# Attention kept on chip, paired heads on both halves of the array, and token-major expert outputs

## The chip, the cores and the metric

One core of one Trainium2 chip. The metric is the device time of one execution in microseconds, the median of several runs. A second number is the span of one profiled execution, from its first to its last instruction.

## The reference, cut to what matters

Inputs are q, k, v of shape 8 x 12 x 448 x 64 (batch, heads, sequence, head size), two scale vectors of 64, a gate matrix (768 x 8), one dense pair of weights (768 x 512, 512 x 768) and eight expert pairs of the same shapes. Everything is float32.

```python
q_n, k_n = rmsnorm(q, g_q), rmsnorm(k, g_k)
attn = softmax(q_n @ k_n.T / sqrt(64))
x = (attn @ v), heads side by side, as (3584 tokens, 768)
y_dense = relu(x @ w1_dense) @ w2_dense
expert = argmax(x @ w_gate);  gate = softmax(x @ w_gate)[expert]
out = y_dense + gate * (relu(x @ w1[expert]) @ w2[expert])
```

Both kernels compute every expert for every token and weigh the result with the gate, which is zero for the experts not chosen.

## The kernel before

It has one function, in which the Tile framework sets the semaphores and orders each engine's queue by the order of the program and the buffers of the pools.

**Attention** (lines 90 to 144) goes batch by batch. For q and k of one batch (12 heads, 5376 rows, 42 rows on each of 128 partitions) it loads f32 (line 96), squares, sums, inverts and takes the root (lines 98 to 102), multiplies by the factor and by g (lines 105, 107), pads to 128 columns and writes bf16 to DRAM (line 109). v is only cast and written (lines 111 to 114). Then two transposing DMAs read q and k back with the head size on the partitions (lines 118, 119), and v comes back with a column of ones (lines 121, 122). For each head there are four score matmuls of 64 x 112 by 448 columns (line 131), each with an exponential on ScalarE (line 132), and for each of four blocks of 112 queries four matmuls of 112 x 112 weights by 65 columns (line 137), a copy out of PSUM (line 139), and the division by the sum in the 65th column (lines 141, 142). The batch's result goes to DRAM (line 144).

**Change-over and gate.** The result comes back transposed as `xc` (line 156). The gate matrix is the stationary operand, so the logits have experts on the partitions (line 161); maximum and sum over them are all-reduces on POOL (lines 166, 172); the gate goes to DRAM (line 179).

**Expert layers** (lines 182 to 220). For the dense pair and each expert, w1t and w2t are loaded through POOL's queue into a pool with one buffer (lines 186, 188). For each of seven blocks of 512 tokens, 24 matmuls make the hidden layer (line 200), which is rectified and multiplied by the gate (line 205; line 209 for the dense pair), and 24 more make the output with features on the partitions (line 214), which VectorE adds to `yacc` (line 220).

**Output** (lines 225 to 231). `yacc` is transposed in f32 in 168 blocks of 128 x 128, each copied (line 230) and written by a DMA of its own (line 231).

Of the kernel before, what the change touches and what calls it, by code (L numbers as in the profile page):

```python
# [14 lines left out]
RO = bass_isa.ReduceOp  # L15
# [3 lines left out]
def kernel(  # L19
# [16 lines left out]

# [4 lines left out]
    F = moe_w1_dense.shape[1]  # L41

    SC = 112
    NSC = S // SC
    scale = 1.0 / (D ** 0.5)
    KD = Dm // P
    NC = 512
    NNC = N // NC
    FT = F // P
    DT = Dm // P  # L50

    xbuf = nc.dram_tensor("x_scratch", (N, Dm), BF16).ap()
    DP = 128
    qn = nc.dram_tensor("qn_scratch", (B * H * S, DP), BF16).ap()
    kn = nc.dram_tensor("kn_scratch", (B * H * S, DP), BF16).ap()
    vn = nc.dram_tensor("vn_scratch", (B * H * S, D), BF16).ap()
    gmask = nc.dram_tensor("gmask_scratch", (E, N), F32).ap()

    const_pool = ctx.enter_context(tc.tile_pool(name="const", bufs=1))
    ident = const_pool.tile([P, P], BF16)  # L60
    make_identity(nc, ident)
    gq_t = const_pool.tile([SC, D], F32)
    gk_t = const_pool.tile([SC, D], F32)
    nc.sync.dma_start(gq_t, bass.AP(tensor=g_q.tensor, offset=g_q.offset, ap=[[0, SC], [1, D]]))
    nc.sync.dma_start(gk_t, bass.AP(tensor=g_k.tensor, offset=g_k.offset, ap=[[0, SC], [1, D]]))
    eps_t = const_pool.tile([P, 1], F32)
    nc.vector.memset(eps_t, 1e-6)

    gq_b = const_pool.tile([P, D], F32)
    gk_b = const_pool.tile([P, D], F32)  # L70
    nc.sync.dma_start(gq_b, bass.AP(tensor=g_q.tensor, offset=g_q.offset, ap=[[0, P], [1, D]]))
    nc.sync.dma_start(gk_b, bass.AP(tensor=g_k.tensor, offset=g_k.offset, ap=[[0, P], [1, D]]))
    BHS = B * H * S
    assert BHS % P == 0
    NBHS = BHS // P
    CH = H * S // P
    assert CH * P == H * S
    qv = q.rearrange("b h s d -> (b h s) d").rearrange("(c p) d -> p c d", p=P)
    kv = k.rearrange("b h s d -> (b h s) d").rearrange("(c p) d -> p c d", p=P)
    vv = v.rearrange("b h s d -> (b h s) d").rearrange("(c p) d -> p c d", p=P)  # L80
    qn_v = qn.rearrange("(c p) d -> p c d", p=P)
    kn_v = kn.rearrange("(c p) d -> p c d", p=P)
    vn_v = vn.rearrange("(c p) d -> p c d", p=P)
# [178 lines left out]
```

## Time and profile before

| | us |
|---|---|
| median of 3 runs (lowest, highest) | 1605.18 (1605.03, 1608.18) |
| span of the profiled execution | 1605.4 |
| TensorE matmuls busy | 1119.3 |
| VectorE busy | 712.4 |
| ScalarE busy | 327.6 |
| GpSimd busy | 97.5 |

Busy time is the union of an engine's instruction records. A matmul's record lasts longer than its share of the engine, because matmuls are pipelined, so the spacing of matmuls says more than their duration. PE is TensorE, PEld its weight loads, DVE VectorE, ACT ScalarE, POOL GpSimd, SP the engine that issues most DMAs. On the timeline and in the chain, a line merges a row of equal instructions: start, length from the first start to the last end, and how many.

### The profile page before, as it was taken

Reading aid. Unit: us, or ns where it says so; the run is one execution under the profiler, and the core shown is the slowest. Engines: PE = TensorE matmul, PEld = TensorE weight load, DVE = VectorE, ACT = ScalarE, POOL = GpSimd, SP = SyncE. Lnnn points to the kernel's source line nnn. Section 1 sums busy time; section 2 is a strip of 40 time slices with the busy share of each in tenths; the row PEclk is TensorE's granted clock in tenths of the full one; section 3 lists DMA queues with packets and bytes.
Section 4 is the critical chain, followed back from the end, with each engine's and each line's share of the span. In section 5 each row is a group of like instructions: output and inputs, shape, how many; then the busy total and the mean of one; then the engine's idle time right before and its main releaser. Section 6 shows DMA issues by size and latency. Waiting matters only on the chain.

```text
span 1605.4 us, 13421 instructions
## 1 busy us (share of the span) xinstructions
PE 1119.3 (70%) x5093; PEld 553.6 (34%) x5154; DVE 712.4 (44%) x1205; ACT 327.6 (20%) x747; POOL 97.5 (6%) x97
## 2 busy tenths in 40 slices
PE   0283719091826455375699989898989898989765
PEld 0151406050413333241244434343434343434322
DVE  6442524445262717120833646464646464645100
ACT  1242515151523334240441000000000000000333
POOL 0000000000000000001710000000000000000000
PEclk9999999999999999999899999999999999999655
DMA  8949394968869493819002020202020202020233
GB/s 175 194 84 173 64 190 86 183 110 156 136 110 182 78 210 51 144 18 177 2 2 40 1 40 1 40 1 40 1 40 1 40 1 40 1 40 1 82 97 97
DMA packets 394064, 125.49 MB, mean 78 GB/s; under 512 B 328656, under 2 KB 393936, under 8 KB 393992
## 3 DMA queue, kind: packets, MB, share of 16 engines
q1 hardware_dynamic: 381408, 110.47, 37.5%
q0 software_dynamic: 12592, 14.17, 6.0%
q8 instruction: 40, 0.66, 0.2%
q14 instruction: 24, 0.20, 0.0%
HBM read 67.11 MB, written 44.15 MB: 69 GB/s over the span
## 4 chain that ended last, share of the span: by engine, by line
PE 52%; DMA 23%; SPq 9%; DVE 7%; issue 4%; ACT 3%; POOL 2%; ACTq 0%; POOLq 0%; DVEq 0%
PE yp L214 17%; PE hp L200 16%; PE out_ps L137 10%; PE sc_ps L131 9%; DMA out_dram<-od 5%; DMA va<-vn_scratch 5%; SPq L118 4%; DMA w1t<-in_moe_w_dram 4%; DMA qn_scratch<-xn 4%; DMA w2t<-in_moe_w_dram 3%; SPq L119 3%; DVE xn L107 2%; DVE ssq L100 2%; SPq L156 2%; DVE xn L105 1%
## 5 line engine op out<-in xcount | busy, mean ns | idle before, releaser
L131 PE MATMUL sc_ps<-qTa,kTa 64*112 64x448 bf16 x384 | 197.7, 594 | 324.6 <-DMA kTa<-kn_scratch 318.7
L214 PE MATMUL yp<-ht,w2t 128*128 128x512 bf16 x1479 | 353.7, 386 | 30.7 <-ACT logits L164 11.2
L200 PE MATMUL hp<-xc,w1t 128*128 128x512 bf16 x1484 | 352.2, 385 | 30.8 <-DMA w1t<-in_moe_w_dram 28.9
L205 DVE SCALAR_TENSOR_TENSOR ht<-hp,gsc 128x512 bf16<-128x512 f32 x224 | 145.4, 686 | 240.6 <-PE yp L214 214.9
L220 DVE TENSOR_TENSOR yacc<-yacc,yp 128x512 f32<-128x512 f32 x336 | 205.9, 682 | 54.0 <-PE yp L214 54.0
L132 ACT ACTIVATE ex<-sc_ps 112x448 bf16<-112x448 f32 x384 | 189.7, 551 | 179.3 <-PE sc_ps L131 179.3
L200 PEld LDWEIGHTS <-w1t 128*128 128x128 bf16 x1512 | 149.9, 99 | 219.1 <-DMA w1t<-in_moe_w_dram 32.8
L214 PEld LDWEIGHTS <-w2t 128*128 128x128 bf16 x1512 | 148.6, 99 | 219.0 <-issue 39.8
L137 PE MATMUL out_ps<-va,ex 112*112 112x65 bf16 x1536 | 186.8, 284 | 31.4 <-DVE va L122 22.9
L137 PEld LDWEIGHTS <-ex 112*112 112x112 bf16 x1536 | 160.1, 206 | 130.9 <-issue 91.4
L230 ACT COPY od<-pT 128x128 f32<-128x128 f32 x168 | 44.2, 266 | 704.8 <-PE pT L228 639.9
L131 PEld LDWEIGHTS <-kTa 64*112 64x112 bf16 x384 | 61.6, 182 | 360.2 <-DMA kTa<-kn_scratch 319.7
L139 DVE COPY out_all<-out_ps 112x65 f32<-112x65 f32 x302 | 57.0, 221 | 163.2 <-PE out_ps L137 157.6
L228 PE MATMUL pT<-ident,yacc 128*128 128x128 f32 x168 | 74.2, 458 | 31.6 <-ACT od L230 29.8
L195 POOL PARTITION_BROADCAST gsc<-g x56 | 44.5, 796 | 492.9 <-DVE ht L205 483.9
L122 DVE MEMSET va<- 112x48 bf16 x8 | 0.8, 98 | 153.5 <-DMA va<-vn_scratch 153.5
L228 PEld LDWEIGHTS pT<-ident,yacc 128*128 128x128 f32 x168 | 29.8, 178 | 76.1 <-ACT od L230 74.0
L98 DVE TENSOR_TENSOR sq<-xt 128x2688 f32<-128x2688 f32 x16 | 47.1, 2941 | 10.2 <-DMA xt<-in_q_dram 10.2
L132 ACT ACT_TABLE_LOAD x8 | 10.3, 1283 | 190.5 <-PE sc_ps L131 190.4
L105 DVE TENSOR_TENSOR xn<-xt,ssq 128x2688 bf16<-128x2688 f32 x16 | 47.3, 2955 | 2.7 <-ACT ssq L102 2.7
L100 DVE TENSOR_REDUCE ssq<-sq 128x42 f32<-128x2688 f32 x16 | 47.1, 2945 | 0.1
L153 POOL DMA_DIRECT2D wgb<-in_moe_w_gate_dram x1 | 1.1, 1137 | 711.9 <-DMA x_scratch<-ob_a 711.9
(37 smaller groups left out, 342.3 us busy)
## 6 DMA issues: line engine op xcount, KB each, us to landing
qn_scratch<-xn SPq DMA_DIRECT2D x8, 1344.0 KB
kn_scratch<-xn SPq DMA_DIRECT2D x8, 1344.0 KB
out_dram<-od SPq DMA_DIRECT2D x168, 64.0 KB
w1t<-in_moe_w_dram POOLq DMA_DIRECT2D x8, 768.0 KB, 7.4
w2t<-in_moe_w_dram POOLq DMA_DIRECT2D x8, 768.0 KB, 6.9
vn_scratch<-xn SPq DMA_DIRECT2D x8, 672.0 KB
va<-vn_scratch SPq DMA_DIRECT2D x8, 672.0 KB
x_scratch<-ob_a SPq DMA_DIRECT2D x8, 672.0 KB
```

The source lines that it names most:

```text
L100: nc.vector.tensor_reduce(ssq, sq, AX.X, ALU.add)
L105: nc.vector.tensor_mul(xn[:, :, :D], xt, ssq.unsqueeze(2).to_broadcast([P, CH, D]))
L118: nc.sync.dma_start(qTa, qn3[b], transpose=True)
L131: nc.tensor.matmul(sc_ps, kT[:, j * SC:(j + 1) * SC], qT, start=True, stop=True)
L132: nc.scalar.activation(ex[:, j, :], sc_ps, AF.Exp, scale=scale)
L137: nc.tensor.matmul(out_ps, ex[:, j, mi * SC:(mi + 1) * SC], va[:, h, j, :], start=(j == 0), stop=(j == NSC - 1))
L139: nc.any.tensor_copy(out_all[:, mi, :], out_ps)
L200: nc.tensor.matmul(hp, w1t[:, kk, ff * P:(ff + 1) * P], xc[:, kk, nj * NC:(nj + 1) * NC], start=(kk == 0), stop=(kk == KD - 1))
L205: nc.vector.scalar_tensor_tensor(ht, in0=hp, scalar=0.0, in1=gsc, op0=ALU.max, op1=ALU.mult)
L214: nc.tensor.matmul(yp, w2t[:, ff, dd * P:(dd + 1) * P], hts[ff], start=(ff == 0), stop=(ff == FT - 1))
L220: nc.vector.tensor_add(ysl, ysl, yp)
L228: nc.tensor.transpose(pT, yacc[:, dd, nn * P:(nn + 1) * P], ident32)
```

## The change

Attention no longer goes through DRAM. Its unit is a pair of heads; there are 48. q and k are loaded with 112 partitions and four tokens each (`load`, six heads at a time), squared on POOL and summed on VectorE (`squares`), and the inverse root is taken as exp(-0.5 ln) on ScalarE for six heads at once (`rnorm`). `normalise` writes bf16 with the two heads side by side, and `transposes` turns both at once on TensorE, so that one head stands on partitions 0 to 63 and the other on 64 to 127; g_q times g_k is multiplied in as q leaves PSUM. `scores` runs two matmuls of 64 rows, one on each half, into two PSUM banks, and one exponential takes both. `attend` uses blocks of 128 queries as weights (the last block overlaps the third by 64). `divide` and `xtrans` put the result into `xc` on chip. The loop runs scores of pair t+1, attend of pair t, the transposed result of t-1 and the transposes of t+2 in turn. Score buffers are two, the accumulator `av` is one.

The gate has tokens on the partitions and is worked out in small VectorE operations, without POOL and DRAM. The expert layers have two weight buffers; the hidden layer is made per batch of 448 tokens, rectified on ScalarE, and is then the stationary operand, 112 tokens at a time, so that the output is token-major: 32 matmuls of 384 columns per batch. The gate is applied in the accumulation on VectorE. The output needs no transposes: in the last expert each batch is written by one DMA as it is done.

The core of the diff (blank lines and small parts left out):

```diff
-                nc.sync.dma_start(dst[:, off:off + CH, :], xn)
...
-            nc.sync.dma_start(qTa, qn3[b], transpose=True)
-            nc.sync.dma_start(kTa, kn3[b], transpose=True)
...
-            nc.sync.dma_start(dst.rearrange("(j s) h d -> s h j d", s=SC), ob_a)
...
-            nc.sync.dma_start(xc[:, kk, :], xbuf[:, kk * P:(kk + 1) * P], transpose=True)
...
-                nc.tensor.transpose(pT, yacc[:, dd, nn * P:(nn + 1) * P], ident32)
...
-                nc.sync.dma_start(out[nn * P:(nn + 1) * P, dd * P:(dd + 1) * P], od)
...
+    JJ = 4
+    SC = S // JJ
+    NPR = H // 2
+    NT = B * NPR
+    GP = 3
+    KD = Dm // P
+    FT = F // P
+    De = D + 1
     scale = 1.0 / (D ** 0.5)
+    QC = (0, 128, 256, S - 128)
...
+    gqk = const.tile([P, 1], F32)
+    nc.vector.tensor_mul(gqk, gq2, gk2)
+    xcp = ctx.enter_context(tc.tile_pool(name="xc", bufs=1))
+    xc = xcp.tile([P, KD, N], BF16)
+    with tc.tile_pool(name="a_ld", bufs=3) as ld, \
+         tc.tile_pool(name="a_sb", bufs=3) as sb, \
+         tc.tile_pool(name="a_sc", bufs=2, space=bass.MemoryType.PSUM) as scp, \
+         tc.tile_pool(name="a_av", bufs=1, space=bass.MemoryType.PSUM) as avp, \
+         tc.tile_pool(name="a_tr", bufs=2, space=bass.MemoryType.PSUM) as trp:
+        xin, ssqs, rs, xn, qkT, exs, vas, xnats = {}, {}, {}, {}, {}, {}, {}, {}
+        def load(g):
+            b, h0 = divmod(g * GP * 2, H)
+            for name, src in (("q", q), ("k", k)):
+                t = ld.tile([SC, 2 * GP, JJ * D], F32, tag="x" + name)
+                nc.sync.dma_start(
+                    t, src[b, h0:h0 + 2 * GP].rearrange("h (p j) d -> p h (j d)", j=JJ))
+                xin[name, g] = t
+            ssqs[g] = sb.tile([SC, 2, 2 * GP * JJ], F32, tag="ssq", name="ssq")
+        def load_v(b):
+            vr = ld.tile([SC, H, JJ * D], BF16, tag="vr", bufs=2)
+            nc.gpsimd.dma_start(vr, v[b].rearrange("h (p j) d -> p h (j d)", j=JJ))
+            va = ld.tile([SC, H, JJ, D + 2], BF16, tag="va", bufs=2)
             nc.vector.memset(va[:, :, :, D:], 1.0)
+            nc.vector.tensor_copy(va[:, :, :, :D], vr.rearrange("p h (j d) -> p h j d", d=D))
+            vas[b] = va
+        def squares(t):
+            g, i = divmod(t, GP)
+            for n, name in enumerate("qk"):
+                x = xin[name, g][:, 2 * i:2 * i + 2, :]
+                sq = sb.tile([SC, 2, JJ * D], F32, tag="sq")
+                nc.gpsimd.tensor_mul(sq, x, x)
+                nc.vector.tensor_reduce(
+                    ssqs[g][:, n, 2 * i * JJ:(2 * i + 2) * JJ],
+                    sq.rearrange("p h (j d) -> p (h j) d", d=D), AX.X, ALU.add)
+        def rnorm(g):
+            r = sb.tile([SC, 2, 2 * GP * JJ], F32, tag="r", name="r")
+            nc.scalar.activation(r, ssqs[g], AF.Ln, bias=eps_t[:SC], scale=1.0 / D)
+            nc.scalar.activation(r, r, AF.Exp, scale=-0.5)
+            rs[g] = r
+        def normalise(t):
+            g, i = divmod(t, GP)
+            for n, name in enumerate("qk"):
+                x = xin[name, g][:, 2 * i:2 * i + 2, :]
+                y = sb.tile([SC, JJ, 2, D], BF16, tag="xn" + name)
+                nc.vector.tensor_mul(
+                    y.rearrange("p j h d -> p h j d"), x.rearrange("p h (j d) -> p h j d", d=D),
+                    rs[g][:, n, 2 * i * JJ:(2 * i + 2) * JJ]
+                    .rearrange("p (h j) -> p h j", j=JJ).unsqueeze(3).to_broadcast([SC, 2, JJ, D]))
+                xn[name, t] = y
+        def transposes(t):
+            for name in "qk":
+                ps = trp.tile([P, S], BF16, tag="tr")
+                for j in range(JJ):
+                    nc.tensor.transpose(ps[:, j * SC:(j + 1) * SC],
+                                        xn[name, t][:, j].rearrange("p h d -> p (h d)"),
+                                        ident[:SC, :SC])
+                y = sb.tile([P, S], BF16, tag="T" + name)
+                if name == "q":
+                    nc.vector.tensor_scalar(y, ps, gqk, None, op0=ALU.mult)
+                else:
+                    nc.vector.tensor_copy(y, ps)
+                qkT[name, t] = y
+        def scores(t, j):
+            if j == 0:
+                exs[t] = sb.tile([SC, JJ, 2, S], BF16, tag="ex", name="ex")
+            ps = scp.tile([SC, 2, 512], F32, tag="sc")
+            for hh in range(2):
+                d0 = hh * D
+                nc.tensor.matmul(ps[:, hh, :S], qkT["k", t][d0:d0 + D, j * SC:(j + 1) * SC],
+                                 qkT["q", t][d0:d0 + D, :], start=True, stop=True)
+            nc.scalar.activation(exs[t][:, j], ps[:, :, :S], AF.Exp, scale=scale)
+        av = {}
+        def attend(t, part):
+            b, pr = divmod(t, NPR)
+            if part == 0:
+                av[t] = avp.tile([P, 2, 512], F32, tag="av", name="av")
+            hh, m0 = divmod(part * 2, 4)
+            for mi in (m0, m0 + 1):
+                for j in range(JJ):
+                    nc.tensor.matmul(av[t][:, hh, mi * De:(mi + 1) * De],
+                                     exs[t][:, j, hh, QC[mi]:QC[mi] + P],
+                                     vas[b][:, 2 * pr + hh, j, :De],
+                                     start=(j == 0), stop=(j == JJ - 1))
+        def divide(t):
+            a4 = av[t][:, :, :4 * De].rearrange("p h (m e) -> p h m e", e=De)
+            inv = sb.tile([P, 2, 4, 1], F32, tag="inv")
+            nc.vector.reciprocal(inv, a4[:, :, :, D:])
+            xa = sb.tile([P, 4, 2, D], BF16, tag="xa")
+            nc.vector.tensor_mul(xa.rearrange("p m h d -> p h m d"), a4[:, :, :, :D],
+                                 inv.to_broadcast([P, 2, 4, D]))
+            xnats[t] = xa
+        def xtrans(t):
+            b, pr = divmod(t, NPR)
+            ps = trp.tile([P, S], BF16, tag="tr")
+            for mi in range(4):
+                nc.tensor.transpose(ps[:, QC[mi]:QC[mi] + P],
+                                    xnats[t][:, mi].rearrange("p h d -> p (h d)"), ident)
+            nc.scalar.copy(xc[:, pr, b * S:(b + 1) * S], ps)
+        def norm_ahead(t):
+            if t < NT:
+                g, i = divmod(t, GP)
+                if i == 0:
+                    load(g)
+                    if g % 2 == 0:
+                        load_v(t // NPR)
+                squares(t)
+                if i == GP - 1:
+                    rnorm(g)
+        for t in range(2 * GP):
+            norm_ahead(t)
+        for t in range(3):
+            normalise(t)
+        for t in range(2):
+            transposes(t)
+        for j in range(JJ):
+            scores(0, j)
+        for t in range(NT + 1):
+            norm_ahead(t + 2 * GP)
+            if t + 3 < NT:
+                normalise(t + 3)
+            for j in range(JJ):
+                if t + 1 < NT:
+                    scores(t + 1, j)
+                if t < NT:
+                    attend(t, j)
+                if j == 1 and t > 0:
+                    xtrans(t - 1)
+                if j == 2 and t + 2 < NT:
+                    transposes(t + 2)
+            if t < NT:
+                divide(t)
+    NTT = N // SC
     with tc.tile_pool(name="m_sb", bufs=3) as sb, \
+         tc.tile_pool(name="m_ps", bufs=4, space=bass.MemoryType.PSUM) as ps1, \
+         tc.tile_pool(name="m_py", bufs=2, space=bass.MemoryType.PSUM) as ps2, \
+         tc.tile_pool(name="m_y", bufs=1) as yp, \
+         tc.tile_pool(name="m_w", bufs=2) as wp:
+        wgb = yp.tile([P, KD, E], BF16)
         nc.gpsimd.dma_start(wgb, moe_w_gate.rearrange("(ko p) e -> p ko e", p=P))
+        lg = yp.tile([SC, NTT, E], F32)
+        for n0 in range(0, NTT, 8):
+            lp = ps1.tile([SC, 8, E], F32, tag="h")
+            for n in range(8):
+                for kk in range(KD):
+                    nc.tensor.matmul(lp[:, n], xc[:, kk, (n0 + n) * SC:(n0 + n + 1) * SC],
+                                     wgb[:, kk, :], start=(kk == 0), stop=(kk == KD - 1))
+            nc.vector.tensor_copy(lg[:, n0:n0 + 8], lp)
...
+        gate = yp.tile([SC, NTT, 1], F32)
+        nc.vector.reciprocal(gate, sm)
+        hot = yp.tile([SC, NTT, E], F32)
+        nc.vector.tensor_scalar(hot, cent, 0.0, None, op0=ALU.is_equal)
+        left = yp.tile([SC, NTT, 1], F32)
+        nc.vector.tensor_copy(left, gate)
+        ge = yp.tile([SC, NTT, E], F32)
+        for e in range(E):
+            nc.vector.tensor_mul(ge[:, :, e:e + 1], hot[:, :, e:e + 1], left)
+            nc.vector.tensor_sub(left, left, ge[:, :, e:e + 1])
+        yacc = yp.tile([SC, NTT, Dm], F32)
+        ov = out.rearrange("(b p j) d -> b p j d", b=B, j=JJ)
+        HD = Dm // 2
         for e in range(-1, E):
             w1v = moe_w1_dense if e < 0 else moe_w1[e]
             w2v = moe_w2_dense if e < 0 else moe_w2[e]
+            w1t = wp.tile([P, KD, F], BF16, tag="w1t")
             nc.gpsimd.dma_start(w1t, w1v.rearrange("(ko p) f -> p ko f", p=P))
+            w2t = wp.tile([P, FT, Dm], BF16, tag="w2t")
             nc.gpsimd.dma_start(w2t, w2v.rearrange("(fo p) d -> p fo d", p=P))
+            for b in range(B):
+                ht = sb.tile([P, FT, S], BF16, tag="ht")
                 for ff in range(FT):
+                    hp = ps1.tile([P, S], F32, tag="h")
                     for kk in range(KD):
                         nc.tensor.matmul(hp, w1t[:, kk, ff * P:(ff + 1) * P],
+                                         xc[:, kk, b * S:(b + 1) * S],
                                          start=(kk == 0), stop=(kk == KD - 1))
+                    nc.scalar.activation(ht[:, ff], hp, AF.Relu)
+                for j in range(JJ):
+                    n = b * JJ + j
+                    yps = ps2.tile([SC, 2, 512], F32, tag="y")
+                    for ff in range(FT):
+                        for dd in range(2):
+                            nc.tensor.matmul(yps[:, dd, :HD], ht[:, ff, j * SC:(j + 1) * SC],
+                                             w2t[:, ff, dd * HD:(dd + 1) * HD],
+                                             start=(ff == 0), stop=(ff == FT - 1))
+                    yv = yacc[:, n].rearrange("p (a d) -> p a d", a=2)
+                    if e < 0:
+                        nc.vector.tensor_copy(yv, yps[:, :, :HD])
                     else:
+                        nc.vector.scalar_tensor_tensor(yv, in0=yps[:, :, :HD],
+                                                       scalar=ge[:, n, e:e + 1], in1=yv,
+                                                       op0=ALU.mult, op1=ALU.add)
+                if e == E - 1:
+                    nc.sync.dma_start(ov[b], yacc[:, b * JJ:(b + 1) * JJ])
```

## Rows read from the trace of the kernel before

**Rows 1.** The page's head.
```profile
span 1605.4 us, 13421 instructions
```
**Rows 2.** Stages: us, busy PE, PEld, DVE, ACT, POOL; granted clock, DMA share, GB/s.
```profile
64.00:711.00 647.00, 354.93 (x1904) 220.08 (x1904) 269.33 (x574) 236.47 (x495) 0.00 (x0) 1.00 0.73 126
...
759.00:1491.00 732.00, 670.75 (x2956) 297.12 (x3015) 395.05 (x599) 39.35 (x73) 92.90 (x86) 0.97 0.12 18
1491.00:1606.00 115.00, 74.83 (x172) 29.95 (x170) 3.67 (x6) 43.94 (x167) 0.00 (x0) 0.53 0.34 96
```
**Rows 3.** The chain, between two batches: start, us, what.
```profile
551.16 9.49 DMA qn_scratch<-xn
...
576.07 9.57 DMA va<-vn_scratch
```
**Rows 4.** The timeline of PE, 502 to 509 us.
```profile
502.50 0.62 PE L131 MATMUL sc_ps<-qTa,kTa 64*112 64x448 bf16 x1
503.05 0.59 PE L137 MATMUL out_ps<-va,ex 112*112 112x65 bf16 x4
503.57 0.62 PE L131 MATMUL sc_ps<-qTa,kTa 64*112 64x448 bf16 x1
...
507.12 0.99 PE L131 MATMUL sc_ps<-qTa,kTa 64*112 64x448 bf16 x2
508.04 0.30 PE L137 MATMUL out_ps<-va,ex 112*112 112x65 bf16 x1
```
**Rows 5.** The timeline of PE at 65 us and at 500 us.
```profile
64.74 3.98 PE L131 MATMUL sc_ps<-qTa,kTa 64*112 64x448 bf16 x10 [64.74 <-DMA kTa<-kn_scratch]
...
499.83 2.74 PE L137 MATMUL out_ps<-va,ex 112*112 112x65 bf16 x28 [2.42 <-DVE va L122]
```
**Rows 6.** Groups of instructions by line and shape: busy us, mean ns of one.
```profile
L220 DVE TENSOR_TENSOR yacc<-yacc,yp 128x512 f32<-128x512 f32 x336 | 205.9, 682 | 54.0 <-PE yp L214 54.0
...
L132 ACT ACTIVATE ex<-sc_ps 112x448 bf16<-112x448 f32 x384 | 189.7, 551 | 179.3 <-PE sc_ps L131 179.3
...
L137 PEld LDWEIGHTS <-ex 112*112 112x112 bf16 x1536 | 160.1, 206 | 130.9 <-issue 91.4 <-DMA va<-vn_scratch 26.5 <-ACT ex L132 13.0
...
L200 PEld LDWEIGHTS <-w1t 128*128 128x128 bf16 x1512 | 149.9, 99 | 219.1 <-DMA w1t<-in_moe_w_dram 32.8 <-issue 15.2
...
L139 DVE COPY out_all<-out_ps 112x65 f32<-112x65 f32 x302 | 57.0, 221 | 163.2 <-PE out_ps L137 157.6
...
L100 DVE TENSOR_REDUCE ssq<-sq 128x42 f32<-128x2688 f32 x16 | 47.1, 2945 | 0.1
...
L195 POOL PARTITION_BROADCAST gsc<-g x56 | 44.5, 796 | 492.9 <-DVE ht L205 483.9 <-DMA g<-gmask_scratch 9.0
...
L172 POOL PARTITION_ALL_REDUCE sm<-ex x7 | 23.8, 3407 | 17.7 <-ACT ex L170 17.7
...
L102 ACT ACT_TABLE_LOAD x8 | 10.3, 1283 | 0.8 <-PEq L246 0.7
...
L132 ACT ACT_TABLE_LOAD x8 | 10.3, 1283 | 190.5 <-PE sc_ps L131 190.4
```
**Rows 7.** The timeline of PE, 1184 to 1196 us.
```profile
1186.70 4.91 PE L200 MATMUL hp<-xc,w1t 128*128 128x512 bf16 x22
...
1195.85 0.38 PE L214 MATMUL yp<-ht,w2t 128*128 128x512 bf16 x1
```
**Rows 8.** Who waited for whom: us in total, times, longest us.
```profile
PE hp L200 <- DMA w1t<-in_moe_w_dram: 28.9, 8, 4.0
```
**Rows 9.** Stage 0 to 80 us, and DMAs with us to landing.
```profile
0.00:80.00 80.00, 10.90 (x60) 7.22 (x61) 44.77 (x35) 12.34 (x20) 1.07 (x8) 1.00 0.98 184
...
w1t<-in_moe_w_dense_dram POOLq DMA_DIRECT2D x1, 768.0 KB, 10.1
wgb<-in_moe_w_gate_dram POOLq DMA_DIRECT2D x1, 12.0 KB, 6.3
```
**Rows 10.** The timeline of ACT, 144 to 150 us.
```profile
146.05 4.45 ACT L132 ACTIVATE ex<-sc_ps 112x448 bf16<-112x448 f32 x10
```

More of the change, by code (lines that the diff above doesn't have):

```diff
@@ L5 @@
 from concourse import mybir
-from concourse import bass_isa
 from concourse.masks import make_identity
@@ L69 @@
[L69 to L79, printed above, removed]
@@ L147 @@
-    with tc.tile_pool(name="m_sb", bufs=3) as sb, \
-         tc.tile_pool(name="m_ps", bufs=8, space=bass.MemoryType.PSUM) as ps, \
-         tc.tile_pool(name="m_xc", bufs=1) as xcp, \
-         tc.tile_pool(name="m_wc", bufs=1) as wcp, \
-         tc.tile_pool(name="m_gc", bufs=1) as gcp:
-        wgb = sb.tile([P, KD, E], BF16, tag="wgb")
-        nc.gpsimd.dma_start(wgb, moe_w_gate.rearrange("(ko p) e -> p ko e", p=P))
-        xc = xcp.tile([P, KD, N], BF16)
-        for kk in range(KD):
-            nc.sync.dma_start(xc[:, kk, :], xbuf[:, kk * P:(kk + 1) * P], transpose=True)
-        for nj in range(NNC):
-            lp = ps.tile([E, NC], F32, tag="p")
-            for kk in range(KD):
-                nc.tensor.matmul(lp, wgb[:, kk, :], xc[:, kk, nj * NC:(nj + 1) * NC],
-                                 start=(kk == 0), stop=(kk == KD - 1))
-            logits = sb.tile([E, NC], F32, tag="logits")
-            nc.any.tensor_copy(logits, lp)
-            mx = sb.tile([E, NC], F32, tag="mx")
-            nc.gpsimd.partition_all_reduce(mx, logits, E, RO.max)
-            cent = sb.tile([E, NC], F32, tag="cent")
-            nc.vector.tensor_sub(cent, logits, mx)
-            ex = sb.tile([E, NC], F32, tag="exg")
-            nc.scalar.activation(ex, cent, AF.Exp)
-            sm = sb.tile([E, NC], F32, tag="smg")
-            nc.gpsimd.partition_all_reduce(sm, ex, E, RO.add)
-            nc.vector.reciprocal(sm, sm)
-            nc.vector.tensor_mul(ex, ex, sm)
-            mask = sb.tile([E, NC], F32, tag="mask")
-            nc.vector.tensor_tensor(mask, logits, mx, ALU.is_equal)
-            gm = sb.tile([E, NC], F32, tag="gm")
-            nc.vector.tensor_mul(gm, mask, ex)
-            nc.sync.dma_start(gmask[:, nj * NC:(nj + 1) * NC], gm)
-        yacc = xcp.tile([P, KD, N], F32, tag="yacc")
@@ new lines @@
+    gqk = const.tile([P, 1], F32)
[20 more added lines that the diff above has]
+            va = ld.tile([SC, H, JJ, D + 2], BF16, tag="va", bufs=2)
+            nc.vector.memset(va[:, :, :, D:], 1.0)
+            nc.vector.tensor_copy(va[:, :, :, :D], vr.rearrange("p h (j d) -> p h j d", d=D))
[41 more added lines that the diff above has]
+            ps = scp.tile([SC, 2, 512], F32, tag="sc")
+            for hh in range(2):
+                d0 = hh * D
[62 more added lines that the diff above has]
+                divide(t)
@@ L210 @@
-                    hts.append(ht)
-                for dd in range(DT):
-                    yp = ps.tile([P, NC], F32, tag="p")
-                    for ff in range(FT):
-                        nc.tensor.matmul(yp, w2t[:, ff, dd * P:(dd + 1) * P], hts[ff],
-                                         start=(ff == 0), stop=(ff == FT - 1))
-                    ysl = yacc[:, dd, nj * NC:(nj + 1) * NC]
-                    if e < 0:
-                        nc.any.tensor_copy(ysl, yp)
-                    else:
-                        nc.vector.tensor_add(ysl, ysl, yp)
```

119 lines of the change are left out of this document (15 added, 104 removed).

## The prediction

> **What bounds the kernel now.** I read the page's head, then the busy time by stage, then the chain of waits, then single matmuls on the timeline, because the stages have different limits. The profiled execution spans 1605.4 us [rows 1]; the median of the runs shown is 1605.18 us, so the sum below is made against 1605.4 and carried over unchanged.
>
> By stage [rows 2] the span falls into a start of 64 us, attention of 647 us, a change-over of 48 us, the expert layers of 732 us and an output stage of 115 us. In attention TensorE is busy 355 of 647 us. The chain shows why: from 551.16 us, where a scratch write of 9.5 begins, to 585.64, where the re-read of v ends, 34.5 us pass with the two transposing DMAs between them and no matmul [rows 3]. This comes once in each of the eight batches. In the remaining part TensorE is the limit, but not by its columns. One score matmul of 448 columns holds the engine 0.55 us until the next full-height matmul starts (502.50 to 503.05), and four 65-column matmuls with their way back into the scores take 0.52 (503.05 to 503.57) [rows 4]. In a row, ten scores take 3.98 us against 0.62 for one, 0.373 us each, and 28 of the 65-column matmuls take 2.74 against 0.30, 0.090 each [rows 5]. 448 columns in 0.373 us is the 1.2 GHz level, though the windows view prints a granted clock of 1.00 there; I go by the spacing. The 0.090 is not the 65 columns (0.054 at that level) but the load of 112 weight columns: its record is 206 ns, while a load of 128 columns has 99 [rows 6]. In the expert layers 22 matmuls take 4.91 us against 0.38 for one, 0.2157 each or 0.421 ns per column [rows 7]: the 2.4 GHz level, nothing else in the way. 3024 of them are 652 of the 732 us; the waits for the weights are in the rest (28.9 us for w1t alone [rows 8]). The output stage runs transposes at a clock of 0.53 in step with small writes [rows 2].
>
> **Removed.** The scratch round trips, the transposing DMAs, the gate's trip through DRAM, the single-buffered weights, and the output stage as a stage. I don't subtract these; each stage is rebuilt.
>
> **Start.** q and k of six heads and v of a batch are 2.75 MB; at the 184 GB/s of the first 80 us [rows 9] that is 15 us, q and k alone about 11 with their issue. Then come six squares on POOL (about 1.2 us each, below), Ln, Exp and table loads (3), normalise, transposes and their copies (3.5) and the first scores with their exponentials (4.5). Sum 30 us, against 64.7 before.
>
> **Attention, 48 head pairs.** TensorE per pair: four times a score pair and eight attend matmuls, plus 8 + 4 transposes.
> - Score pair: one score is 0.55. The second sits on the other 64 rows. At best it adds its load, 0.09; at worst it runs behind the first, 0.373 (two scores went 507.12 to 508.04, 0.92 [rows 4]). No row shows two row groups at once; I take 0.64, since banks and rows differ. [...]
> - Eight attend matmuls now load 128 columns. Four take 0.52 now: the last begins 0.29 after the first (record 0.59 less 0.30 for one) and 0.23 before the next score. Eight are then 7 x 0.054 + 0.23 = 0.61 if the 65 columns bind, or 7 x 0.09 + 0.23 = 0.86 if loads bind as now. I take 0.61, since the 128-column load record is half as long [rows 6].
> - Four turns: 5.0. Transposes: 896 and 512 columns at 1.2 GHz, 1.18.
> - The single accumulator av: the last attend's result is out 0.30 after its start (the record of one [rows 4]), then DVE runs a reciprocal of eight elements (0.2, as the copy of 65) and a 512-element product (0.68 [rows 6]): 1.18. TensorE has 0.23 + 0.64 to fill it with: a wait of 0.31.
> Sum 6.49, say 6.5 us.
>
> ACT per pair: exponentials of 896 columns; ten of 448 take 4.45 us, 0.434 apart [rows 10], so 0.87 each, 3.5 for four; a copy of 448, 0.43; Ln and Exp of the norms, 48 elements each, some 0.25 each (an exponential of 448 is 0.55 [rows 6]) in one pair of three, 0.16. Table loads: Sqrt and Exp alternate now and 16 loads stand in the trace, two a batch, 1283 ns each [rows 6]. I carry this over to Ln and Exp: two loads for each of 16 groups, 0.86 per pair. ACT 4.95. In the one pair of three that has the loads ACT needs 3.93 + 0.5 + 2.57 = 7.0, over TensorE's 6.5; with the wait for the sums in its queue I put 0.7 us, 16 times, 11 us in all. [...]
>
> DVE per pair, from 2945 ns for 2688 elements, 682 for 512 and 221 for 65 [rows 6]: two sums of squares 1.1, two products 1.1, two copies out of PSUM 1.2, the division 0.85, a share of the v copy 0.3. That is 4.6, hidden. POOL's squares, two of 512 elements, have no row. The nearest are a broadcast of 512 (0.8 us) and an all-reduce of 512 (3.4) [rows 6], 1.6 to 6.8 per pair; I take 1.2 each, near the broadcast, since no partition is crossed, but with a second operand to read. Hidden; at the upper end 0.3 per pair shows, 14 us. The v copy waits on DVE's queue for a POOL DMA; POOL reaches that DMA some two pairs earlier, 13 us against about 10 for a cast transfer that size [rows 9], so nothing; without that lead up to 8 us for each of seven batches. Input of 33 MB at 184 GB/s is 180 us, beside the work.
>
> Attention: 48 x 6.5 + 11 = 323 us.
>
> **Change-over.** Last division and transposes 3; the gate weights wait for attention's buffers as now, then issue 1 and landing 6.3 [rows 9]; 192 gate matmuls at the 112-column load, 0.09 each, 17; 1 of rest. w1t lands (10.1) inside that. The gate's small operations on DVE, some 25 of 0.1 to 0.4 us, run beside the dense pair's matmuls, which don't read the gate. Sum 28, between 17 (loaded early) and 48 (as now).
>
> **Expert layers.** 1728 matmuls of 448 columns and 2304 of 384 at 0.421 ns a column: 326 + 373 = 699 us, 47 us over the 652 now, since 112 tokens fill seven eighths of the array's columns. The 384-column ones load 112 columns: 0.09 against 0.162 of streaming, so hidden, as the score loads are behind 0.373 [rows 5]. Bounds: 0; 44 ns each (record 206 less 162), 101 us; all 90 on top, 207 us. I take 0. Relu of 448 takes about what the exponential does, 0.55 [rows 6], and is wanted six matmuls, 1 us, later; DVE adds 768 elements in about 0.95 (682 ns for 512, and 256 more) every 1.3 us. Both hidden, the second with 0.15 to spare (if gone, 2 x 72 x 0.1 = 14 us). The weights' second buffer lets an expert's load, 10 us, run beside the 78 us of the expert before; POOL's queue holds nothing else by then: 0. Clock ramp 4. Sum 703.
>
> **End.** The writes of the first seven batches, 7.5 us each, lie beside 9.7 us of matmuls each. Last addition 1; 1.38 MB at 184 GB/s, 7.5; fixed part 2.5. Sum 11.
>
> 30 + 323 + 28 + 703 + 11 = **1095 us**.
>
> **Rivals.**
> - *The score pair runs serially* (the row tiling does nothing): 0.28 x 4 more per pair, less the 0.28 of the av wait that it covers, 48 times, and less the 11 of ACT: 1095 + 40 - 11 = 1124. For it: no row of two row groups.
> - *TensorE gets 2.4 GHz in attention*: per pair the streaming halves (0.19 less per score pair, 0.19 per eight attends, 0.59 for the transposes) and the av wait grows by some 0.3, so TensorE is near 4.7 and ACT's 4.95 binds; with the two interlocked I put 5.2: 1095 - 323 + 250 = 1022. For it: fewer holes than in the 86 us batches. Against: ten scores back to back stayed at 0.373 [rows 5].
> - *The 112-column loads show in the expert layers*: 1196 to 1302. For it: the 0.090 row. Against: the 0.373 row.
> - *Slower than before*: the expert layers run at 1.2 GHz, if shorter matmuls with more loads between them don't hold the higher level. All of it would add 699, 1794 us; over 1605 from 73% of the stage on. Against: the stage has 0.97 now, with worse gaps than the change leaves [rows 2].
>
> **How the numbers follow.** Forecast 0.50, serial pair 0.17, higher clock 0.20, loads shown 0.10, lower level 0.02, no measurable change 0.01. Around the forecast itself the bounds (attend loads +48, POOL +14, v copy +56, change-over -11 to +20, addition +14, tables -11) give about 1075 to 1165. The range 1015 to 1210 takes in the higher clock, the serial pair and the smaller load case. 0.2%, 3 us, is about what a measurement can tell from none: faster 0.97, same 0.01, slower 0.02.
>
> **What would show it.** Right: score pairs starting within 0.1 us, attends 0.054 apart, 32 extra table loads, attention ending near 353 us, hp 0.189 and yps 0.162 apart, a tail near 11 us. Wrong: attends 0.09 apart, starts of a pair 0.37 apart, DVE or POOL busy over 90% in attention, yps 0.2 or 0.25 apart.

## The result and the profile after

The changed kernel takes **1080.39 us** (median of four runs, 1078.99 to 1081.8) against 1606.68 (1605.03 to 1609.43) for the kernel before on the same chip: ratio 0.6721, 95% interval [0.671, 0.6732]. Forecast: 1095, range 1015 to 1210. The profiled execution spans 1078.2 us. A ratio leaves out single runs that lie more than 1.5% above the fastest run of their kernel, which happens only in experiment 2.

The page's head, beside [rows 1]:

```profile
span 1078.2 us, 15442 instructions
PE 985.4 (91%) x6720; PEld 651.4 (60%) x6720; DVE 505.5 (47%) x716; ACT 395.5 (37%) x593; POOL 129.4 (12%) x129
...
PEclk9999956656657699999999999999999999999999
```

TensorE is busy for 91% of a span that is a third shorter. The line PEclk is the granted clock in 40 slices of 27 us: it is below full in slices 6 to 14, most of attention and the change-over. The first five slices print 9, but the matmuls there are as slow as where the lower level is granted. The first change on record comes at 128 us; before it, two scores of a pair take 0.62 us, as they do later in a stretch with a granted clock of 0.51 (135 to 166 us), and in one with 1.00 (166 to 176) they take 0.40:

```profile
89.41 0.62 PE L137 MATMUL ps<-y 64*112 64x448 bf16 x2
...
174.44 0.40 PE L137 MATMUL ps<-y 64*112 64x448 bf16 x2 [2.64 <-ACT ex L139]
```

No view prints a frequency: the 1.2 and 2.4 GHz of the prediction are estimates of mine, columns per nanosecond worked out from its spacings (448 columns in 0.373 us, one in 0.421 ns).

The stages, beside [rows 2] (start:end, length, busy time of PE, PEld, DVE, ACT, POOL with instruction counts, granted clock, DMA share, GB/s):

```profile
42.00:346.00 304.00, 260.24 (x2473) 162.13 (x2471) 190.42 (x372) 230.92 (x295) 94.74 (x89) 0.73 0.34 77
346.00:366.00 20.00, 17.59 (x189) 17.62 (x190) 0.67 (x3) 0.00 (x0) 0.18 (x1) 0.51 0.06 2
366.00:1070.00 704.00, 703.79 (x4037) 469.41 (x4036) 296.08 (x311) 156.87 (x289) 11.03 (x14) 1.00 0.15 30
```

So: start 42 us (64 before), attention 303 (647), change-over 21 (48), experts 703.5 (732), end 8.4 (115). Attention gives 344 of the 527 us, the end 107, change-over and experts 55, the start 22.

TensorE's timeline over one pair of heads, beside [rows 4] (start, length to the last end, operation, count, wait and its releaser):

```profile
222.64 0.65 PE L150 MATMUL av<-va,ex 112*128 112x65 bf16 x8
223.10 0.56 PE L121 MATMUL ps<-ident,y 112*128 112x112 bf16 x4
223.59 0.62 PE L137 MATMUL ps<-y 64*112 64x448 bf16 x1
224.14 0.55 PE L121 MATMUL ps<-ident,y 112*128 112x112 bf16 x4
224.63 0.62 PE L137 MATMUL ps<-y 64*112 64x448 bf16 x1
225.18 0.62 PE L150 MATMUL av<-va,ex 112*128 112x65 bf16 x8
225.73 1.15 PE L137 MATMUL ps<-y 64*112 64x448 bf16 x4
227.42 0.62 PE L137 MATMUL ps<-y 64*112 64x448 bf16 x2 [0.55 <-ACT ex L139]
227.97 1.06 PE L150 MATMUL av<-va,ex 112*128 112x65 bf16 x16
228.84 0.62 PE L168 MATMUL ps<-ident,xa 128*128 128x128 bf16 x4
229.25 0.65 PE L150 MATMUL av<-va,ex 112*128 112x65 bf16 x8
```

Two scores of a pair (x2) have the same 0.62 us as one alone, and four have 1.15: the two halves of the array run at once. Eight attends take 0.55 until the next score. The pair takes 6.61 us, of which 0.55 is a wait, not for the accumulator but for the exponentials that empty the two score buffers. Over the whole of attention it is the same (last two numbers: idle time before the group, and what ended most of it):

```profile
L137 PE MATMUL ps<-y 64*112 64x448 bf16 x384 | 127.3, 551 | 36.2 <-ACT ex L139 35.9
...
L150 PE MATMUL av<-va,ex 112*128 112x65 bf16 x1536 | 103.6, 234 | 3.6 <-DVE xa L160 3.6
```

Scores wait 35.9 us for the exponentials, attends 3.6 us for the accumulator. The scheduler didn't keep the program's order score, attend, score, attend: it puts 16 attends together and splits one pair of scores around the transposes.

### The profile page after: what moved, and what is told of

The parts are those of the page before. It is cut to its first block, busy times and chain, and to the rows that moved or that the text cites. A ratio compares the mean times of both kernels' runs of the same rounds, so it can differ in the third digit from the quotient of the medians.

```text
span 1078.2 us, 15442 instructions
## 1 busy us (share of the span) xinstructions
PE 985.4 (91%) x6720; PEld 651.4 (60%) x6720; DVE 505.5 (47%) x716; ACT 395.5 (37%) x593; POOL 129.4 (12%) x129
## 4 chain that ended last, share of the span: by engine, by line
PE 81%; ACT 9%; DMA 4%; DVE 3%; issue 1%; POOL 0%; SPq 0%; ACTq 0%; POOLq 0%; DVEq 0%
PE yps L267 35%; PE hp L258 31%; PE av L150 6%; PE ps L137 6%; ACT ex L139 5%; DMA t<-in_k_dram 3%; PE ps L121 2%; PE lp L220 2%; DVE y L111 2%; PE ps L168 1%; ACT L102 1%; ACT L103 1%; DMA vr<-in_v_dram 1%; DVE ssq L96 1%; ACT xc L170 0%
## 5 line engine op out<-in xcount | busy, mean ns | idle before, releaser
L274 DVE SCALAR_TENSOR_TENSOR yacc<-yps,ge,yacc 112x768 f32<-112x768 f32 x256 | 260.5, 1018 | 362.9 <-PE yps L267 362.9
L267 PE MATMUL yps<-w2t,ht 128*112 128x384 bf16 x2304 | 386.2, 326 | 0.0
L261 ACT ACTIVATE ht<-hp 128x448 bf16<-128x448 f32 x288 | 156.5, 543 | 540.5 <-PE hp L258 540.5
L267 PEld LDWEIGHTS <-ht 128*112 128x112 bf16 x2304 | 299.5, 130 | 81.0
L258 PE MATMUL hp<-xc,w1t 128*128 128x448 bf16 x1728 | 340.7, 354 | 0.0
L139 ACT ACTIVATE ex<-ps 112x896 bf16<-112x896 f32 x192 | 166.2, 915 | 46.1 <-PE ps L137 45.6
L137 PE MATMUL ps<-y 64*112 64x448 bf16 x384 | 127.3, 551 | 36.2 <-ACT ex L139 35.9
L95 POOL TENSOR_TENSOR sq<-t 112x512 f32<-112x512 f32 x96 | 105.8, 1124 | 141.6 <-DMA t<-in_q_dram 107.5
L150 PEld LDWEIGHTS <-ex 112*128 112x128 bf16 x1536 | 84.0, 123 | 57.3 <-issue 52.8
L150 PE MATMUL av<-va,ex 112*128 112x65 bf16 x1536 | 103.6, 234 | 3.6 <-DVE xa L160 3.6
```

Of the source, the lines that this page charges most:

```text
L95: nc.gpsimd.tensor_mul(sq, x, x)
L137: nc.tensor.matmul(ps[:, hh, :S], qkT["k", t][d0:d0 + D, j * SC:(j + 1) * SC], qkT["q", t][d0:d0 + D, :], start=True, stop=True)
L139: nc.scalar.activation(exs[t][:, j], ps[:, :, :S], AF.Exp, scale=scale)
L150: nc.tensor.matmul(av[t][:, hh, mi * De:(mi + 1) * De], exs[t][:, j, hh, QC[mi]:QC[mi] + P], vas[b][:, 2 * pr + hh, j, :De], start=(j == 0 ...
L258: nc.tensor.matmul(hp, w1t[:, kk, ff * P:(ff + 1) * P], xc[:, kk, b * S:(b + 1) * S], start=(kk == 0), stop=(kk == KD - 1))
L261: nc.scalar.activation(ht[:, ff], hp, AF.Relu)
```

## The experiments

Times are medians; ratios are to runs of the kernel before on the same chip. In attention, TensorE's matmuls follow each other in the same order as in the kernel after in experiments 1 to 4 and 11. Experiments 5 and 6 share another order, and 10 and 12 have each their own.

**1. The two heads on the same half of the array.**

```diff
-                d0 = hh * D
+                d0 = 0
```

> The second head of each pair takes its scores from the first head's rows (its own scores are left out), so both score matmuls stand on the same 64 rows and can't run side by side. Theory A (TensorE sets the pace of attention): each of the 192 pairs grows by 0.37 us of streaming, 71 us, of which the wait for av and ScalarE's lateness cover some; 1080 + 30 to 55. Theory B (ScalarE sets it, 5.3 us a pair of heads): TensorE has room, under 1080 + 10. If the row tiling gave nothing: 1080.

1126.62 us, ratio 0.7002 [0.6989, 0.7014]: 46 us more. The same groups on its timeline:

```profile
225.58 0.99 PE L137 MATMUL ps<-y 64*112 64x448 bf16 x2
226.50 0.62 PE L150 MATMUL av<-va,ex 112*128 112x65 bf16 x8
227.05 1.74 PE L137 MATMUL ps<-y 64*112 64x448 bf16 x4
```

Two scores are now 0.99 instead of 0.62, four 1.74 instead of 1.15, which is 0.30 to 0.37 us for each pair of scores; the rival had 0.28. From the fifth pair of heads to the 47th the first attends are 7.27 us apart on average, against 6.34 in the kernel after. The page prints a full clock through attention, but no stretch of it has the spacing of the higher level, so the 46 us also hold what the six stretches at that level were worth. That the two halves run at once is shown.

**2. One function in the norms.** Ln becomes Exp, and the trace has one table load, where that of the kernel after has 32; the logarithm is left out.

```diff
-            nc.scalar.activation(r, ssqs[g], AF.Ln, bias=eps_t[:SC], scale=1.0 / D)
+            nc.scalar.activation(r, ssqs[g], AF.Exp, bias=eps_t[:SC], scale=1.0 / D)
```

> The logarithm of the norm is replaced by an exponential (the norms are then not the reference's), so that one table serves all of attention; the order of the instructions on TensorE and VectorE stays. 31 of 32 table loads go, 40 us of ScalarE. Theory A: 11 us less, as in the forecast, 1069. Theory B (ScalarE sets the pace): 35 to 40 less, 1040 to 1045. If they are hidden altogether: 1080.

Two runs took 1055.35 and 1057.08 us, two 1073.16 and 1073.38; the ratio is that of the first two, 0.6564 [0.6545, 0.6582]. By these the loads cost 24 us. The kept trace is of the run with 1073.16, so what sets the two groups apart isn't shown. Experiments 5 and 6, in another order of TensorE, give 16 us for the same edit. The kernel after has 32 loads, by form (count, busy us, mean ns, idle before):

```profile
L102 ACT ACT_TABLE_LOAD x16 | 20.5, 1283 | 1.0 <-PEq L293 0.7
L103 ACT ACT_TABLE_LOAD x14 | 18.0, 1283 | 0.2
...
L139 ACT ACT_TABLE_LOAD x2 | 2.6, 1283 | 0.0
```

That is 41 us of loads, of which 16 to 24 are on the path; the forecast had 11.

**3. The first batch's v copied later.** In the program only the VectorE copy of v for batch 0 moves, behind the first scores.

```diff
+            if b:
+                copy_v(b)
...
+        copy_v(0)
```

> The first batch's v copy stands in the program after the first scores, not ahead of the first sums of squares; nothing else is moved by hand. Theory A (VectorE's queue stands still until v has landed, 31 us): the first attend comes 10 to 12 us earlier than at 42, 1069. Rival (k, POOL's squares and the norms take that long anyway): 1080.

1079.03 us, ratio 0.6703 [0.6685, 0.6721]: no difference that can be told. The edit didn't take effect: the scheduler put the copy back to where it was, at 10.66 us in this trace and 11.42 in the kernel after. It was the wrong copy besides, as the start of the kernel after shows as a chain of waits:

```profile
4.07 13.00 DMA t<-in_k_dram
...
20.11 11.32 DMA vr<-in_v_dram
...
31.45 0.03 DVE va L87
```

The v that lands at 31.43 us was issued at 20.11. It is the *second* batch's, and its copy stands in VectorE's queue ahead of the first normalise.

**4. Blocks of 128 tokens.** ScalarE's copy into xc puts the tokens in their natural order, and the gate and the experts go by 128 and 512 tokens instead of 112 and 448.

```diff
-            nc.scalar.copy(xc[:, pr, b * S:(b + 1) * S], ps)
+            nc.scalar.copy(xc[:, pr, b * S:(b + 1) * S].rearrange("p (s j) -> p j s", j=JJ),
+                           ps.rearrange("p (j s) -> p j s", s=SC))
...
-    NTT = N // SC
+    TB = P
+    NTT = N // TB
+    NB = 512
```

> Attention's result is written to xc in the order of the tokens (a strided ScalarE copy), and the expert layers take 7 blocks of 512 tokens and 28 of 128, so that the second layer has 2016 matmuls of 384 columns, not 2304, with 128 weight columns. Theory A (columns alone count): 288 x 0.162 = 47 us less, 1033. Rival (the 112-column weight loads cost something too): more than 47 less, and a spacing under 0.162 us. Rival (the strided copy costs ScalarE as much): attention longer by up to 25 us, 1058.

**1031.95 us**, ratio 0.6414 [0.6401, 0.6426], the fastest kernel of this study. The experts take 656 us, 47 less: an eighth of the array's columns was empty, as the forecast worked out. A row of 32 yps takes 5.20 us in both kernels, so the 112-column weight loads cost nothing there. The gate takes 7.35 us instead of 18.05, which I hadn't put in. Attention ends 11 us later; only ScalarE's copy was changed in it, and TensorE's order is the same, so this is the price of the copy. Groups by form and the gate's row in the chain, first of this kernel:

```profile
L223 PEld LDWEIGHTS <-xc 128*128 128x128 bf16 x167 | 4.6, 104 | 6.2 <-issue 6.2
...
L170 ACT COPY xc<-ps 128x448 bf16<-128x448 bf16 x48 | 55.4, 1155 | 26.7 <-PE ps L168 26.7
...
358.85 4.28 PE lp L223 x155
```

then of the kernel after:

```profile
L220 PEld LDWEIGHTS <-xc 128*112 128x112 bf16 x192 | 18.0, 213 | 3.9 <-issue 3.9
...
L170 ACT COPY xc<-ps 128x448 bf16<-128x448 bf16 x48 | 25.5, 532 | 26.2 <-PE ps L168 26.1
...
348.41 18.05 PE lp L220 x192
```

The same copy, with bf16 elements written 8 bytes apart, takes 1155 ns instead of 532. In the gate only 8 columns stream, and the loads show: 94 ns for each matmul with 112 weight columns (192 in 18.05 us), 28 with 128 (155 in 4.28). The granted clock was 0.50 in both gates, and a load's record has 213 ns for 112 columns and 104 for 128.

**5 and 6. A fourth buffer for q and k, with and without Ln.**

```diff
-                t = ld.tile([SC, 2 * GP, JJ * D], F32, tag="x" + name)
+                t = ld.tile([SC, 2 * GP, JJ * D], F32, tag="x" + name, bufs=4)
```

> q and k get four load buffers in place of three, so that a group's load is issued some 19 us earlier. In the changed kernel POOL's squares wait 118 us for loads, VectorE's sums behind them hold up the copies out of PSUM once a batch, and TensorE has a hole of about 5 us there, at whose end its clock falls. Theory A (the late loads cost attention time): 20 to 40 us less, 1040 to 1060, the chain free of the k load, and the stretches at 2.4 GHz longer. Rival B (TensorE at 1.2 GHz makes up for the hole by what is queued): 1080. Rival C (ScalarE then sets the pace, 5.3 us a pair): attention no shorter than 48 x 5.3 = 254 us, against 301 now.

> Four load buffers and no logarithm together (the norms are not the reference's). If the two costs are separate: e5 less 15 us. If ScalarE sets the pace once the loads are early (rival C of e5): e5 less 35 to 40 us, since all 40 us of table loads then lie on the path. If the loads were not on the path: 1065, as with the logarithm alone left out.

1091.16 us, ratio 0.6794 [0.6779, 0.681], *slower* by 11; and 1075.36, 0.6693 [0.668, 0.6706]. My theory, that POOL's wait for q and k sets the pace, falls. Nor was there the hole of 5 us that I had put down: TensorE's longest wait in attention is 2.64 us. POOL's idle time behind q's load went from 107.5 us to 62.0, but the v load at the start took 15.87 us instead of 11.32 and the first attend came at 46.5, 4.5 later, and attention itself took some 5 more, in another order of TensorE's work. The difference between experiments 5 and 6, whose order is the same, is the price of the table loads in it: 16 us.

**7. Token order made on VectorE.** Experiment 4 with the strided write in the copy of q instead.

```diff
-                    nc.vector.tensor_scalar(y, ps, gqk, None, op0=ALU.mult)
+                    nc.vector.tensor_scalar(y.rearrange("p (s j) -> p j s", j=JJ),
+                                            ps.rearrange("p (j s) -> p j s", s=SC),
+                                            gqk, None, op0=ALU.mult)
```

> As the run with 128 tokens, but the order of the tokens is made where VectorE copies q out of PSUM (a strided write of 448), and ScalarE's copy is plain again (532 ns, not 1155). Theory (the strided ScalarE copy cost attention the 11.5 us by which it was longer): 1032 - 11 = 1021. Rival (VectorE's strided write costs the same there): 1032.

1036.13 us, ratio 0.6452 [0.6436, 0.6468]: no better than experiment 4. The copy takes 1214 ns instead of 448:

```profile
L126 DVE TENSOR_SCALAR y<-ps,gqk 128x448 bf16<-128x448 bf16 x46 | 55.8, 1214 | 85.3 <-PE ps L121 85.3
```

**8 and 9. Each half of the change alone.** In 8 the attention of before, with its DRAM trips and transposing loads, feeds the new gate and experts; in 9 the new attention (with the copy of experiment 7) feeds the gate, the experts and the output of before.

```diff
+        xc = yp.tile([P, KD, N], BF16)
         for kk in range(KD):
             nc.sync.dma_start(xc[:, kk, :], xbuf[:, kk * P:(kk + 1) * P], transpose=True)
...
```

> Attention, its scratch tensors and the transposing read of x as before; gate and expert layers as changed. By stages: 711 to the end of attention, 42 for x, 18 for the gate matmuls, 703, 8.5 at the end: 1483. If the expert layers gained from the new attention in some way: more.

> The other half alone: the attention of after, with q's columns put into token order by VectorE's copy (1213 ns for 448 in the run with 128-token blocks, some 13 us in all), and the gate, the expert layers and the output of before. Nothing is left out. If the two halves of the change add up, attention ends near 358, and before's 732 us of experts and 115 us of tail follow a change-over of 5 to 28 us: 1210 to 1233, a saving of 374 to 396 beside the 112 that the new experts alone gave. Rival: the halves overlap (the whole is worth more than its parts because only together does the activation stay on chip and the weights come early): then the change-over stays at before's 48 and the time is 1253 or more.

1494.82 us, ratio 0.9304 [0.9279, 0.9329], and 1213.0, 0.7538 [0.7523, 0.7553]. Against 1606.3 and 1608.0 beside them that is 112 and 395; experiment 9's attention ended at 360 us instead of 345 for its strided copy, so that half is worth 410 without it. 112 + 410 = 522 of the 526 of the whole: the halves add up, within some 10 us. Experiment 9 came out as expected. Experiment 8 took 12 us more than the 1483 put down: the last transposed piece of x landed at 764.45 us, where 753 had been put (753.48 in the kernel before), and the gate's matmuls wait for it. In 9 the old output stage is back:

```profile
758.21 6.24 DMA xc<-x_scratch
764.49 16.22 PE lp L164 x172
```

```profile
1094.00:1212.00 118.00, 76.92 (x183) 31.07 (x181) 4.37 (x7) 43.81 (x168) 0.00 (x0) 0.53 0.31 94
```

**10 and 12. q loaded in token order; v loaded later.** 12 moves only the calls that load v, each with its DMA and its VectorE copy; 10 has that and the 128-token blocks with q's order made by its load, in pieces of 256 bytes.

```diff
-                    if g % 2 == 0:
-                        load_v(t // NPR)
...
+            if t == 0:
+                load_v(0)
...
+            if t % NPR == 2 and t // NPR + 1 < B:
+                load_v(t // NPR + 1)
```

> Token blocks of 128 without a strided copy: q is loaded in token order by its DMA in pieces of 256 bytes instead of 1 KB, and the v copies of the later batches come later. Nothing is left out. Theory: the copies go back to 448 and 532 ns, experts 656 and gate 7 as in the run with 128-token blocks, attention 303 less 5 for the start: 1015 to 1025. Rival: the smaller pieces make q's load later than the 9 to 13 us that the k load now takes at each batch, TensorE's hole once per group of pairs grows, and attention takes 315 or more: 1032 or more, no better than the strided ACT copy.

> Only the order of the v loads: the first batch's v is loaded behind the first q and k, each later batch's in the middle of the batch before, so that no v copy of the second batch stands in VectorE's queue ahead of the first normalise. Nothing is left out. Theory: VectorE's idle stretch of 5.6 us before that copy goes from the start chain; first attend near 36 instead of 42, time near 1075. Rival: what follows in the start is then late on its own account (the first k load takes 13 us, then squares and the 4 table loads), first attend after 40 and the time within 1078 to 1082; slower than 1085 if the later v loads stand in POOL's queue ahead of squares in the steady state.

12: 1103.78 us, ratio 0.6861 [0.685, 0.6871], 23 *slower*. 10: 1041.08, 0.647 [0.6458, 0.6483]. 10 came out as its rival had it, 1032 or more. For 12 only the rival's last clause holds, slower than 1085: POOL waited 26.0 us in front of the v loads, 16.3 in the kernel after, but whether this made attention longer isn't shown. The first attend came at 40.8, 1.2 us earlier: I had put the first v behind POOL's first squares, so it was late itself (landed at 30.2). And attention went from 303 to 328 us. The page prints a full clock until 360 us, but until then the spacing is that of the lower level, with 6.5, 6.5, 8.3 us for three pairs over and over: the pair that has the table loads pays 1.8 us each time. ScalarE around them in 12:

```profile
201.97 1.28 ACT L102 ACT_TABLE_LOAD   x1
...
203.62 1.28 ACT L139 ACT_TABLE_LOAD   x1
```

and in the kernel after, where the pair with the loads took 6.8 us and the next 5.5:

```profile
190.06 1.28 ACT L102 ACT_TABLE_LOAD   x1
...
191.60 0.51 ACT L170 COPY xc<-ps 128x448 bf16<-128x448 bf16 x1
192.13 1.28 ACT L103 ACT_TABLE_LOAD   x1
```

The loads are the same; what stands around them isn't. After has a useful copy between them, 12 has the exponentials at once, and TensorE's order differs too. Which of these costs the 1.8 us, and why the clock stays low, no run here separates. 10 is 62.7 us faster than 12, about the 58 that experiment 4 gained in experts and gate, so the small pieces of q's load show no cost (it landed in 4.8 us at the median, 5.4 in 12), though TensorE's order differs between the two. That load with after's v order was not run; the parts would put it near 1022, an estimate.

**11. One weight buffer.**

```diff
-         tc.tile_pool(name="m_w", bufs=2) as wp:
+         tc.tile_pool(name="m_w", bufs=1) as wp:
```

> One buffer for each expert's weights instead of two; nothing is left out. The forecast put the weight loads at nothing because a second buffer hides them behind 78 us of matmuls. If that cover is what hides them, each of 8 experts now waits: w1t is free when the last hp is done, lands 7.4 us and an issue of 0.8 later, while 32 yps take 5.2; w2t is free after these and lands 7.5 to 9 later while 24 hp take 4.5. Some 5 us for each of 8, 40 in all, and up to as much again if the clock falls in the holes: 1110 to 1160. Rival: the scheduler finds other matmuls to fill the wait, or the loads come in time: below 1090.

1118.41 us, ratio 0.6951 [0.6937, 0.6964]: 38 us more, for eight experts: from one expert's first matmul to the next one's it is 82.7 us instead of 77.9. One of them on TensorE's timeline:

```profile
441.33 5.36 PE L267 MATMUL yps<-w2t,ht 128*112 128x384 bf16 x32
449.08 6.40 PE L258 MATMUL hp<-xc,w1t 128*128 128x448 bf16 x24 [2.39 <-DMA w1t<-in_moe_w_dram]
455.78 5.38 PE L267 MATMUL yps<-w2t,ht 128*112 128x384 bf16 x32 [0.30 <-DMA w2t<-in_moe_w_dram]
```

The waits are 2.4 us for w1t and 0.3 for w2t, and the 24 matmuls between them take 6.40 us instead of 4.70, since the granted clock fell behind the hole (3.4 us at the lower level, recorded from 449.5). So it goes in six of the eight. In the other two no lower clock is recorded, the 24 take 4.71, and the wait for w2t is 1.9 and 2.3 us instead. The zero that the forecast put on the loads rests on the second buffer, and this is its price.

## Why the prediction was right

- **Attention, 6.5 us a pair.** Pair by pair, from first attend to first attend, the 20 pairs that lie wholly in stretches recorded at the lower clock are 6.34 us apart on average. In the pair shown the sum was right with another split: 6.18 of TensorE and 0.31 of waiting for av were forecast, 6.06 and 0.55 of waiting for ScalarE were measured. The 0.64 for a score pair (0.55 to 0.62), the 0.61 for eight attends (0.55) and the 0.054 between attends (0.055: 16 in 1.06 us, where one has 0.24) all came out at the right end of their bounds. The half-length load record that spoke for 0.61 was weak evidence, since it set 206 ns at the lower clock beside 99 at the higher; experiment 4 has both at the lower, 213 and 104. That the accumulator binds is the step that failed: the scheduler's order fills that wait, and the score buffers bind.
- **Attention as a whole, 323 against 303.** The first four pairs took 30.3 us, 3 more than their share of 6.73 each. The last four took 15.5, 11 less: the last two pairs have no transposes of q and k left to run and the last no next scores, which the forecast forgot, and a stretch at the higher clock covers the last three. The 40 between took 257.4, 12 less. What makes up the 12 stays open. It isn't the table loads, whose term was too small (11 against 16 to 24), so the rest of the pair was put too high; nor do the stretches at the higher clock explain it, since all 42 pairs from the fifth to the 47th, these stretches included, are also 6.34 us apart on average. No run that keeps both functions shows the 11 us less that the prediction's bounds allow for the tables: the kernel after has 32 loads, and experiment 2, with one load and 24 us less, leaves the logarithm out.
- **Start, 30 against 42.** Mis-sized. k took 13.0 us to land beside the other loads, and then the second batch's v copy, which I had costed only for the steady state, stood in VectorE's queue until 31.4. Experiments 3 and 12 didn't free the start, each for a reason of its own, so what it would be without that copy stays open.
- **Change-over, 28 against 21.** The gate matmuls were right (17 forecast, 18.05). The gate weights landed in 2.6 us, not 6.3, with next to nothing else moving (the DMA share is 0.06 in that stretch): the dense pair's weights were issued at 39 to 43 us, in buffers that attention didn't hold.
- **Experts, 703 against 703.5; end, 11 against 8.4.** hp are 0.189 apart and yps 0.162, as written, in the chain's last rows; its first row of hp shows the rise of the clock:

```profile
366.46 6.59 PE hp L258 x24
...
1060.05 4.54 PE hp L258 x24
1064.59 5.21 PE yps L267 x32
...
1069.83 1.02 DVE yacc L274
```

  The rise, put at 4 us without a row, cost 2: the first 24 hp took 6.59 instead of 4.54. The addition took 1.02 us of the 1.3 between two tiles. The forecast's "0.15 to spare" doesn't follow from its own 0.95 and 1.3; measured is 0.28. The write of the last batch took 7.4 us, where 10 were put, 2.5 of them a fixed part for which no row stood. The 112-column loads stay hidden behind 384 columns, and show (94 ns) behind 8, in the gate.
- **Rivals.** The serial pair is excluded by experiment 1. The higher clock in attention came true in part, in six recorded bouts of 7 to 14 us, and did little: the pair that lies wholly in the bout from 166 to 176 us took 6.80, not 5.2, with 3.05 of it waiting for exponentials behind the table loads (the row at 174.44 above has 2.64 of them). Loads showing in the experts and experts at the lower level didn't happen: yps are 0.162 apart, and the stage's row has a granted clock of 1.00.

Measured less forecast is +12, -20, -7, +0.5 and -3, -17 against the span: the late start hid part of what attention did better, so that the total is closer than its terms; that part is luck.

## What to carry to other kernels

A stage whose limit is one engine can be forecast closely from the spacing of its matmuls at the clock that the spacing shows, provided each hidden transfer is checked for the buffer that hides it. The two halves of this change, run alone, add up to the whole within some 10 of 526 us. In an interlocked stage, though, an edit that only means to remove a wait (a buffer, an earlier or later load) can change the scheduler's order, and here two such edits cost 11 and 23 us; a third changed nothing at all, since the scheduler undid it. Measure them, and read the order before the waits.

## What the runs showed that I had not expected

- *Strided writes.* Copies out of PSUM with bf16 elements written 8 bytes apart took 1155 ns instead of 532 on ScalarE and 1214 instead of 448 on VectorE.
- *VectorE beside POOL.* The products of two operands slowed down while POOL was at work, the reductions didn't. First VectorE's timeline, then POOL's:

```profile
41.06 2.79 DVE L111 TENSOR_TENSOR y<-t,r 112x512 bf16<-112x512 f32 x2
43.78 0.67 DVE L96 TENSOR_REDUCE ssq<-sq 112x8 f32<-112x512 f32 x1
...
55.70 0.65 DVE L111 TENSOR_TENSOR y<-t,r 112x512 bf16<-112x512 f32 x1
```

```profile
40.38 2.04 POOL L95 TENSOR_TENSOR sq<-t 112x512 f32<-112x512 f32 x2
...
43.19 2.56 POOL L95 TENSOR_TENSOR sq<-t 112x512 f32<-112x512 f32 x2
...
52.59 3.03 POOL L95 TENSOR_TENSOR sq<-t 112x512 f32<-112x512 f32 x3 [0.48 <-DVE ssq L96]
62.45 1.25 POOL L95 TENSOR_TENSOR sq<-t 112x512 f32<-112x512 f32 x1 [6.82 <-DMA t<-in_q_dram]
```

  With POOL at work beside them (squares, and the issue of a weight load between 42.36 and 43.17) two products take 2.79 us; with POOL idle (55.62 to 62.45) one takes 0.65. A reduction takes 0.67 beside the squares (at 43.78) and 0.67 with POOL idle (at 64.17, between squares that end at 63.70 and begin at 65.21). VectorE is only 63% busy in attention, but at its start these products stand in the chain of waits (2.72 us from 41.14, 2.50 from 45.70), so they may have a part in the 3 us that the first four pairs took too long; no run separates it.
- *The clock in attention.* It rose for single bouts in the kernel after, the first on record at 128 us. With the same order on TensorE the first came at 90.4 us in experiment 3 and at 87.7 in 11, and none in attention in 1. What it follows there stays open.
